# Reading K transposed with odd and even keys alternating, in a grouped-query attention kernel

## The chip, the core and the metric

The kernel runs on one core of one Trainium2 chip. The metric is the device time of one execution in microseconds. A core has five engines that run their own instruction streams and meet at semaphores: TensorE (PE in the profile, with PEld for its weight loads), VectorE (DVE), ScalarE (ACT), GpSimd (POOL) and SyncE (SP), which here issues every DMA. Matmuls write PSUM; the other engines read it and work in SBUF, both 128 partitions wide.

## What is computed

```python
B, Hq, Hkv, Sq, Sk, D = 16, 32, 8, 16, 2048, 128     # q, k, v in bfloat16

def reference(q, k, v):
    rep = Hq // Hkv                                    # 4 query heads share one K/V head
    k = jnp.repeat(k, rep, axis=1)
    v = jnp.repeat(v, rep, axis=1)
    scores = jnp.einsum("bhqd,bhkd->bhqk", q, k) * D ** -0.5
    p = jax.nn.softmax(scores, axis=-1)
    return jnp.einsum("bhqk,bhkd->bhqd", p, v)
```

Four query heads of 16 queries meet the same K and V, so each of the 128 K/V heads has 64 query rows against 2048 keys. K and V are 67 MB each and are read once.

## The kernel before

**Tiling.** Two K/V heads make a pair; there are 64 pairs (NP), and every step handles one pair with 128 query rows, 64 of each head. A chunk is eight pairs (1024 query rows), and Q is loaded and transposed by chunks.

**K.** `load_k` brings a pair's K to `Kn` as one 1 MB transfer; six buffers. A partition holds 32 neighbouring keys of one head with their 128 values, so partitions 0 to 63 are one head and 64 to 127 the other. VectorE (L294) transposes `Kn` in blocks of 32x32 four-byte words, each of which is two neighbouring bf16 values, into `KT`, in two instructions a pair. `KT` then has, for each 32 partitions (half a head), the 32 word positions of a block down the partitions and the keys along the free side. Counted in words the free side is (t b e a x): eight blocks t, two halves b of the head dimension, e for the even or odd key, and 64 positions (a x). Each word holds the two bf16 values of the contraction, and TensorE takes one of them at a time, so it reads with a step of two elements (4 bytes). Two buffers of `KT`.

**Scores.** For a pair, TensorE does 32 matmuls (L250). Four row groups r of 32 rows work at the same time, each for half a head; four accumulation steps `acc` cover the two halves b and the two values in a word; u picks four of the eight blocks t. Each matmul moves 512 columns of `KT` past 64 columns of weights from `QT` and writes 64 partitions of a PSUM bank. `S_ps` has 2048 f32 columns (four banks), in one buffer.

**Negate, minimum, exp.** VectorE (L310) reads `S_ps`, multiplies by minus the softmax scale, takes the row minimum into `nbias` and writes `Sneg` (f32, two buffers), changing the order from half-then-block to block-then-half in runs of 128. ScalarE (L340) computes exp of `Sneg`, with the row sum in `rowsum`, and writes `P` in bf16 (two buffers). `P` is later handled as four-byte words which must hold the even and the odd key side by side; `Sneg` has 64 even keys and then 64 odd ones, so exp reads one of each by turns, 64 words apart, and writes in order.

**Transposes of P, output.** TensorE transposes the words of `P` (L265) in two halves of four blocks to a ring of three PSUM banks `ST_ps`; ScalarE copies each half to `PT` (L350). TensorE multiplies `PT` with V (L281, 32 matmuls), ScalarE divides by the row sum while it copies the result to an output buffer (L360), and SyncE stores it (L199). The reciprocal of the row sum is VectorE's (L301).

**Q.** GpSimd repeats and rearranges a chunk (L163), TensorE transposes it in four parts (L232) in the same PSUM ring, and ScalarE copies each part to `QT` (L330).

**Order.** The order is written out in `pe_prog` and `act_prog`. For pair p, TensorE issues the scores of p+1, the output of p-3, the transposes of p and, for four pairs of each chunk but the last, a part of the next chunk's Q. ScalarE issues exp of p, the scaled copy of p-3, the two copies of P transposed and then the copy of Q. VectorE issues L310 of p, the reciprocal of p-1 and the two K transposes of p+2. The scores of p+1 wait for `sem_max` of p, since `S_ps` has one buffer, and for the K transposes of p+1; L310 waits for the scores; exp of p waits for L310 of p; the transposes of p wait for exp of p. SyncE issues K loads, V loads four pairs later and stores twelve pairs later in one queue. A K load of pair p waits for the transposes of pair p-6, a V load for the output matmuls of pair p-8. The last pair's V comes in two halves.

## Time and profile before

| | |
|---|---|
| time, median of 3 runs | 347.7 us (347.54 to 348.13) |
| profiled execution, its own time | 347.37 us |
| its span, first to last instruction | 345.6 us |
| mean granted clock of TensorE | 0.989 |
| busy: PE / PEld / DVE / ACT / POOL | 278.7 / 193.2 / 295.8 / 280.4 / 30.3 us |
| moved by DMA | 139.11 MB, mean 403 GB/s |
| scores, matmuls of L250 | 2048, 130.2 us |
| exp, L340 | 64, 159.6 us, mean 2494 ns |

The span runs from the first to the last instruction of the profiled execution; its time is a little longer, and the runs without a profile are listed beside it. Busy time is the time in which an engine had an instruction in it. In the page's groups, each row names the source line, engine and operation, output and inputs with their shapes, the count, busy time and the mean duration of one, and, after the second bar, the idle time of the engine just before these instructions and what ended it. Matmuls overlap, so the mean duration of one is longer than the spacing between them. In a timeline, each row gives the start and the length in us of a run of instructions merged into one.

### The profile page before, as it was taken

The page shows a single profiled execution, that of the slowest core. Times are in us where ns is not written, and L with a number is a line of the kernel's source. Part 1 is how long each engine was busy: PE and PEld are TensorE (multiplying, and loading weights), DVE is VectorE, ACT ScalarE, POOL GpSimd, SP SyncE. Part 2 cuts the span into 40 slices and gives each one's busy share as a digit, 9 for nine tenths or more (in the row PEclk, how much of TensorE's full clock was granted, in tenths as well). Part 3 has the DMA queues.
Part 4 walks back from the last instruction along what each step waited for, and adds up shares of the span by engine and source line. Part 5 has one row for each costly group of instructions (what it writes and reads, how often), then busy time and mean ns, then how long its engine had stood idle before and what let it go on. Part 6 is the DMA issues. An engine that isn't in the chain of part 4 may idle for free.

```text
span 345.6 us, 11109 instructions
## 1 busy us (share of the span) xinstructions
PE 278.7 (81%) x4864; PEld 193.2 (56%) x4864; DVE 295.8 (86%) x320; ACT 280.4 (81%) x353; POOL 30.3 (9%) x15
## 2 busy tenths in 40 slices
PE   0667898898999889898869988778877798687785
PEld 0544665665566656666545665456655566454565
DVE  2399989998999989998879989888898898898970
ACT  1458898889988898898866988878987789778776
POOL 4500031000400012000210003000040000000000
PEclk9989999999999999999998999999999999999999
DMA  7999999999999999999999999999999999999983
GB/s 303 423 418 416 407 417 413 412 416 413 413 416 417 416 416 411 418 415 416 414 414 417 415 414 418 412 417 416 414 417 415 414 416 416 414 418 418 408 338 99
DMA packets 37310, 139.11 MB, mean 403 GB/s; under 512 B 11408, under 2 KB 11408, under 8 KB 29072
## 3 DMA queue, kind: packets, MB, share of 16 engines
q1 hardware_dynamic: 37264, 138.42, 98.9%
q8 instruction: 38, 0.62, 0.7%
q14 instruction: 8, 0.07, 0.0%
HBM read 136.31 MB, written 2.10 MB: 401 GB/s over the span
## 4 chain that ended last, share of the span: by engine, by line
DMA 29%; ACT 22%; PE 17%; DVE 14%; issue 14%; SPq 2%; POOL 1%; ACTq 0%
DMA Kn<-in_k_dram 24%; ACT P L340 14%; PE S_ps L250 9%; DVE Sneg L310 8%; DVE KT L294 6%; ACT PT L350 6%; PE ST_ps L265 5%; DMA out_dram<-O 4%; PE O_ps L281 2%; ACT QT L330 2%; SPq L199 2%; DMA Qn<-in_q_dram 1%; POOL Q L163 1%; ACT O L360 1%; PE S_ps L281 0%
## 5 line engine op out<-in xcount | busy, mean ns | idle before, releaser
L294 DVE STREAM_TRANSPOSE KT<-Kn 128x1024 f32<-128x1024 f32 x128 | 151.3, 1221 | 27.6 <-DMA Kn<-in_k_dram 27.5
L340 ACT ACTIVATE P<-Sneg,nbias 128x2048 bf16<-128x2048 f32 x64 | 159.6, 2494 | 12.8 <-DVE Sneg L310 12.4
L250 PE MATMUL S_ps<-KT,QT 32*64 32x512 bf16 x2048 | 130.2, 390 | 36.8 <-DVE Sneg L310 32.5
L310 DVE TENSOR_SCALAR_CACHE_REDUCE Sneg<-S_ps 128x2048 f32<-128x2048 f32 x64 | 144.7, 2262 | 14.0 <-PE S_ps L250 13.7
L250 PEld LDWEIGHTS S_ps<-KT,QT 32*64 32x64 bf16 x2048 | 61.2, 104 | 85.6 <-issue 48.2
L350 ACT ACTIVATE PT<-ST_ps 128x512 f32<-128x512 f32 x128 | 69.6, 595 | 24.2 <-PE ST_ps L265 24.2
L265 PE MATMUL ST_ps<-ident,P 128*128 128x128 f32 x512 | 70.7, 282 | 16.7 <-ACT P L340 16.4
L281 PEld LDWEIGHTS O_ps<-Vb,PT 128*64 128x64 bf16 x1952 | 56.4, 110 | 26.3 <-issue 26.3
L265 PEld LDWEIGHTS ST_ps<-ident,P 128*128 128x128 f32 x512 | 55.5, 142 | 26.4 <-ACT P L340 24.0
L281 PE MATMUL O_ps<-Vb,PT 128*64 128x128 bf16 x1952 | 66.2, 221 | 0.0
L163 POOL COPY Q<-Qn 128x4096 bf16<-128x4096 bf16 x8 | 28.8, 3600 | 228.1 <-DMA Qn<-in_q_dram 157.6
L330 ACT ACTIVATE QT<-ST_ps 128x1024 bf16<-128x1024 bf16 x32 | 32.7, 1032 | 9.0 <-PE ST_ps L232 9.0
L360 ACT ACTIVATE O<-O_ps,rrec 128x128 bf16<-128x128 f32 x61 | 22.5, 370 | 15.0 <-PE O_ps L281 14.8
L232 PE MATMUL ST_ps<-ident,Q 128*128 128x128 bf16 x256 | 20.6, 231 | 10.0 <-POOL Q L163 10.0
L232 PEld LDWEIGHTS ST_ps<-ident,Q 128*128 128x128 bf16 x256 | 18.2, 104 | 10.3 <-issue 9.9
L340 ACT ACTIVATION_READ_ACCUMULATOR P<-Sneg,nbias 128x1 f32 x64 | 13.0, 203 | 0.0
L301 DVE RECIPROCAL rrec<-rowsum 128x1 f32<-128x1 f32 x64 | 10.1, 158 | 2.8 <-ACT P L340 2.8
L310 DVE DVE_READ_ACCUMULATOR Sneg<-S_ps 128x1 f32 x64 | 5.3, 83 | 0.0
L281 PE MATMUL S_ps<-Vb,PT 128*64 128x128 bf16 x96 | 3.1, 220 | 0.7 <-ACT PT L350 0.7
L281 PEld LDWEIGHTS S_ps<-Vb,PT 128*64 128x64 bf16 x96 | 2.8, 110 | 1.0 <-ACT PT L350 1.0
L360 ACT ACTIVATE O<-S_ps,rrec 128x128 bf16<-128x128 f32 x3 | 1.0, 368 | 1.2 <-PE S_ps L281 1.2
L330 ACT ACT_TABLE_LOAD x1 | 1.3, 1283 | 0.7 <-PEq L375 0.7
(7 smaller groups left out, 1.7 us busy)
## 6 DMA issues: line engine op xcount, KB each, us to landing
Kn<-in_k_dram SPq DMA_DIRECT2D x64, 1024.0 KB, 16.5
Vb<-in_v_dram SPq DMA_DIRECT2D x63, 1024.0 KB, 18.1
Qn<-in_q_dram SPq DMA_DIRECT2D x8, 256.0 KB, 16.0
out_dram<-O SPq DMA_DIRECT2D x64, 32.0 KB, 16.0
Vb<-in_v_dram SPq DMA_DIRECT2D x2, 512.0 KB, 12.5
```

Of the source, the lines that this page charges most:

```text
L163: gp.tensor_copy(Q4[:, :, :, :, :].rearrange("p j b r x -> p (j b) r x"), src.unsqueeze(2).to_broadcast([128, 16, 4, 64]),).then_inc(sem_q ...
L232: ins = pe.transpose(dst[:, 128 * j:128 * (j + 1)], src[:, j, b, e, :], ident[:, :])
L250: ins = pe.matmul(S_ps[64 * g:64 * (g + 1), 512 * (2 * h + u):512 * (2 * h + u + 1)], qt[rows, acc, 128 * i + 64 * g:128 * i + 64 * (g + 1 ...
L265: ins = pe.transpose(dst[:, 128 * t:128 * (t + 1)], P[p % 2][:, 128 * x:128 * (x + 1)], ident4[:, :])
L281: ins = pe.matmul(o_ap(p)[64 * g:64 * (g + 1), :], pt[:, j // 2, j % 2, 64 * g:64 * (g + 1)], Vb[p % NV][:, g, j, :], start=(j == 0), stop ...
L294: dve.transpose(KT[p % NKT][:, :].rearrange("p (t b e a x) -> p x e t b a", t=J // 2, b=2, e=2, x=2)[:, x, :, :, :, :], Kn[p % NK][:, :].b ...
L301: dve.reciprocal(rrec[:, p:p + 1], rowsum[:, p:p + 1]).then_inc(sem_rec, 1)
L310: dve.tensor_scalar(Sneg[p % 2][:, :].rearrange("p (t h x) -> p h t x", t=8, h=2), S_ps[:, :].rearrange("p (h t x) -> p h t x", t=8, h=2), ...
L330: act.activation(QT[c % 2][:, i, :].rearrange("p (a j) -> p a j", j=8), stage_ap(u).bitcast(BF16).rearrange("p (j a) -> p a j", j=8), ACT. ...
L340: act.activation(P[p % 2][:, :].bitcast(BF16).rearrange("p (n y e) -> p n y e", n=16, e=2), Sneg[p % 2][:, :].rearrange("p (n e y) -> p n ...
L350: act.activation(PT[p % NPT][:, 4 * h:4 * (h + 1), :].rearrange("p t q -> p (t q)"), stage_ap(u), ACT.Copy,).then_inc(sem_ev, 1)
L360: act.activation(Osb[p % NO][:, :], o_ap(p), ACT.Copy, scale=rrec[:, p:p + 1]).then_inc(sem_nm, 1)
```

## The change

The scores' matmuls read the same 512 columns in another order, and exp's access patterns become plain. `KT` itself, the weights, the PSUM columns written, L310 and all that follows exp stay as they are.

```diff
-                    kt = KT[p % NKT][:, :].bitcast(BF16).rearrange("p (t b y e) -> p b e t y", t=J // 2, b=2, e=2)
+                    kt = KT[p % NKT][:, :].bitcast(BF16).rearrange("p (t b x y e) -> p b e t y x", t=J // 2, b=2, x=2, e=2)
...
-                                    kt[rows, b, e, 4 * u:4 * (u + 1), :],
+                                    kt[rows, b, e, 4 * u:4 * (u + 1), :, :],
...
                     act.activation(
-                        P[p % 2][:, :].bitcast(BF16).rearrange("p (n y e) -> p n y e", n=16, e=2),
-                        Sneg[p % 2][:, :].rearrange("p (n e y) -> p n y e", n=16, e=2), ACT.Exp,
+                        P[p % 2][:, :].bitcast(BF16), Sneg[p % 2][:, :], ACT.Exp,
                         bias=nbias[:, p:p + 1], scale=-1.0, accum_out=rowsum[:, p:p + 1],
                     ).then_inc(sem_exp, 1)
```

In the matmul's pattern, e is now the bf16 value within a word, y one of 64 positions and x the even or odd key. Before, a block's 128 columns were read in memory order, each 4 bytes after the one before. Now x runs fastest: a column of the even half, the column of the odd half at the same position 256 bytes further on, then back to the next of the even half. The scores come to `S_ps`, and through L310 to `Sneg`, with even and odd keys side by side, and exp reads and writes 2048 neighbouring elements.

## The prediction, made before the changed kernel was run

> **What bounds the kernel now.** I read the page's slices and queues first, then the groups of instructions, then the timeline of single pairs. The slices show the engine clock, the DMA share in tenths and the rate; the queue line gives the bytes.

> ```profile
> PEclk9989999999999999999998999999999999999999
> DMA  7999999999999999999999999999999999999983
> GB/s 303 423 418 416 407 417 413 412 416 413 413 416 417 416 416 411 418 415 416 414 414 417 415 414 418 412 417 416 414 417 415 414 416 416 414 418 418 408 338 99
> ...
> q1 hardware_dynamic: 37264, 138.42, 98.9%
> ```

> From the second slice to the thirty-eighth the 16 DMA engines are never under nine tenths and the rate is 407 to 423 GB/s, at most 2% from its middle. The transfers bound the kernel: 139.11 MB over 64 pairs of heads is 2.17 MB a pair, and at 415 GB/s that is 5.2 us a pair. The engines come next, and close behind:

> ```profile
> L294 DVE STREAM_TRANSPOSE KT<-Kn 128x1024 f32<-128x1024 f32 x128 | 151.3, 1221 | 27.6 <-DMA Kn<-in_k_dram 27.5
> L340 ACT ACTIVATE P<-Sneg,nbias 128x2048 bf16<-128x2048 f32 x64 | 159.6, 2494 | 12.8 <-DVE Sneg L310 12.4
> L250 PE MATMUL S_ps<-KT,QT 32*64 32x512 bf16 x2048 | 130.2, 390 | 36.8 <-DVE Sneg L310 32.5
> L310 DVE TENSOR_SCALAR_CACHE_REDUCE Sneg<-S_ps 128x2048 f32<-128x2048 f32 x64 | 144.7, 2262 | 14.0 <-PE S_ps L250 13.7
> ...
> L350 ACT ACTIVATE PT<-ST_ps 128x512 f32<-128x512 f32 x128 | 69.6, 595 | 24.2 <-PE ST_ps L265 24.2
> ...
> L330 ACT ACTIVATE QT<-ST_ps 128x1024 bf16<-128x1024 bf16 x32 | 32.7, 1032 | 9.0 <-PE ST_ps L232 9.0
> L360 ACT ACTIVATE O<-O_ps,rrec 128x128 bf16<-128x128 f32 x61 | 22.5, 370 | 15.0 <-PE O_ps L281 14.8
> ```

> What to see is the waiting columns: the K transposes wait 27.5 us for K loads. Under that lies a loop between two engines. S_ps has one buffer, so the scores of pair p+1 (L250) start only when L310 has read those of pair p, and L310 of p+1 only when they are written:

> ```profile
> 98.67 2.25 DVE L310 TENSOR_SCALAR_CACHE_REDUCE Sneg<-S_ps 128x2048 f32<-128x2048 f32 x1
> ...
> 101.08 2.00 PE L250 MATMUL S_ps<-KT,QT 32*64 32x512 bf16 x32 [0.35 <-DVE Sneg L310]
> 101.30 2.49 ACT L340 ACTIVATE P<-Sneg,nbias 128x2048 bf16<-128x2048 f32 x1
> ...
> 103.20 2.25 DVE L310 TENSOR_SCALAR_CACHE_REDUCE Sneg<-S_ps 128x2048 f32<-128x2048 f32 x1
> ```

> From one L310 to the next is 4.53 us, of which the scores are 2.00. Call this time of a pair's 32 matmuls T. They run four at a time on different row groups, so T is 8 rounds of 250 ns, each moving 512 columns: 0.488 ns a column. One pair in the trace ran with TensorE's clock at half (0.50 in the window from 182 to 184 us) and shows the loop with a longer T:

> ```profile
> 180.82 3.54 PE L250 MATMUL S_ps<-KT,QT 32*64 32x512 bf16 x32 [1.99 <-DVE Sneg L310]
> ...
> 184.41 2.29 DVE L310 TENSOR_SCALAR_CACHE_REDUCE Sneg<-S_ps 128x2048 f32<-128x2048 f32 x1 [0.81 <-PE S_ps L250]
> ...
> 186.86 2.00 PE L250 MATMUL S_ps<-KT,QT 32*64 32x512 bf16 x32 [0.45 <-DVE Sneg L310]
> ```

> L310 began 0.05 us after the scores ended (184.36), and the next scores began 2.50 us after that end. Whatever T is, the loop is T + 2.50.

> **The change, part by part.** No instruction, wait, transfer or buffer is added, removed or moved. Two access patterns change.

> Exp (L340) loses the step in its read. Its price without it comes from ACT's other rows: 512 elements take 595 ns and 1024 take 1032, so 0.854 ns an element and 158 ns fixed; L360's 128 elements with a per-partition operand take 370, 103 more than 158 + 109. So 2048 elements should take 158 + 103 + 1749 = 2010 ns, against 2494: 484 ns saved in each, 31 us of ACT in all. With the step, exp pays (2494 - 261)/2048 = 1.09 ns an element. All but the last exp are hidden behind the transfers; if that cover went, the loop above, without ACT in it, would be next. The last one lies on the path to the end: from it to the end come L360, L350, L281 and the store, so 0.48 us. The halves of the last V were issued at 327.6 and 328.6 us and took 12.4 to 12.6 to land, so by 341.2; its matmuls, now at 341.83, could start 0.48 earlier and would wait for the second half only from their middle. The saving stands.

> TensorE takes that step. Each matmul moved 128 neighbouring columns 4 bytes apart, in four blocks; now each two neighbouring columns lie 256 bytes apart (128 bf16), and the next two start 4 bytes on. Instructions, columns, weight loads and what lands in PSUM are as many as before, in contiguous order as before. No row shows such a read on TensorE: its other moving operands (identity, V) have no hop. I bound T from the rows:
> - Lower end: the hop is free, T = 2.00 (row L250).
> - Exp pays 0.236 ns an element for the very same hops (256 bytes there and back), 28% over its own rate. As a ratio on TensorE: T = 2.56. As an added price: 0.724 ns a column, T = 2.97.
> - As a floor in absolute time, if one hopped element cannot be had from SBUF faster than exp gets it: 1.09 ns a column, 558 ns a round, T = 4.46.
> - Upper end: the K transposes, which write every second word, take 1221/1024 = 1.19 ns a word: T = 4.88. A hop added whole to today's column, 0.488 + 1.09 = 1.58, would make T = 6.47.

> I take 4.46. The row is of the same pattern in the same memory, and TensorE asks for a column every 0.42 to 0.49 ns, over twice as often as exp's 0.854: an engine that already loses 28% at its pace says the memory, not the engine, sets the time of a hopped element.

> [...]

> **The sum.** A pair in which TensorE also transposes a part of Q (28 of 64 lie between two scores) has more to do between the scores:

> ```profile
> 145.88 1.08 PE L281 MATMUL O_ps<-Vb,PT 128*64 128x128 bf16 x32
> ...
> 146.89 1.09 PE L265 MATMUL ST_ps<-ident,P 128*128 128x128 f32 x8
> 147.82 0.61 PE L232 MATMUL ST_ps<-ident,Q 128*128 128x128 bf16 x8
> 148.49 2.00 PE L250 MATMUL S_ps<-KT,QT 32*64 32x512 bf16 x32
> ```

> The scores before these ended at 145.95, so 2.54 us between scores. A longer T hides the K transposes (2.35 us) and all of ACT (2.01 + 0.20 + 0.37 + 1.09 + 1.03 = 4.70 us against a loop of 7), and nothing of it comes out between scores, since exp is then done before L265 needs it. The first scores start at 14.95. After the last scores end, at 334.79, comes L310's part of the loop, 2.50, to 337.29, and then 8.31 us to the end of the span at 345.6, 7.83 with the shorter exp. So

> span = 14.95 + 64 T + 36 x 2.50 + 28 x 2.54 + 7.83 = 183.9 + 64 T,

> where the transfers do not set it. T = 2.00 gives 312, well under the 345.6 of the transfers: a cover of 33 us. Break-even is T = 2.53, or 316 ns a round, 26% more than now. T = 4.46 gives 469.3. The profiled execution took 347.37 for a span of 345.6, so 1.77 lie around it: 471.1 us. The median of the runs, 347.7, is 0.33 above that execution, which changes nothing here. The K loads wait for the transposes of pair p-6 and so slow down with the loop; nothing waits for them any more.

> **Rivals.**
> - *The hop costs TensorE nothing that shows* (T up to 2.53). For it: matmuls already read with a 4-byte step and take only about 17% more than 213 ns a round, half of the 0.42 to 0.43 us at which the half-clock pair's rounds follow one another. Against it: exp's 28%. Then the transfers stay the bound and only the last exp is saved: 347.37 - 0.48 = 346.9, or 347.2 against the median. Under 0.2% (0.7 us, about what a measurement of this kernel can tell from no change), so no change; it is faster if the earlier evictions also let SyncE, which waits 42.7 us for L360 before its stores, smooth the stream by another 0.3 us.
> - *A price that partly hides*: ratio or added price, T = 2.56 to 2.97, 349.5 to 375.8 us. It decides from 316 ns a round on. For it: TensorE may fetch ahead over the two streams, as each still moves by 4 bytes.
> - *A price over exp's*: the fetch of the hop added to the column, T = 6.47, 599.7 us. Against it: nothing on the page pays that much for one element.
> - *It doesn't do what it says*: exp's 2494 ns come from elsewhere, its function or its SBUF read, and stay. With the rest as forecast, 471.6; with a free hop, 347.7.

> **Chances.** Price per column between 0.8 and 1.2 ns, so T from 3.28 to 4.92, 395.6 to 500.5 us: 0.62, and 471 is its likeliest point. Partly hidden, 348 to 395: 0.14. Dearer, over 500: 0.09. Nothing that shows, with exp unchanged or not: 0.15, of which 0.08 within 0.2% and 0.07 faster. So slower 0.85. The range leaves out the case of no price (0.15) and the upper part of the dearer one (0.05): 350 to 520.

> **What would show it.** Right: L250's busy time more than doubles, one matmul means about 560 to 700 ns instead of 390, L310 waits over 100 us for L250, DMA falls to seven tenths in the slices and about 300 GB/s, exp falls to about 2010 ns and K transposes wait no more for loads. The step on TensorE's price is wrong if one pair's scores last well under 4 us or above 5; if they stay at 2.0 to 2.5, the page keeps its nines in the DMA row and the prediction is wrong altogether. The step on exp is wrong if L340 stays above 2300 ns.

## The result, and the profile after

The changed kernel takes 474.49 us (median of 4 runs, 473.64 to 474.84) against 347.73: a ratio of 1.364, 95% interval 1.362 to 1.366. The forecast was 471.1. The profiled execution took 474.26 us with a span of 472.5.

The slices of the page after, TensorE's clock, the DMA share in tenths and the rate:

```profile
PEclk9878998999999999899999999989999999999899
DMA  8999988888888887888988887888888888783200
GB/s 333 419 416 413 413 316 290 330 307 294 329 294 312 323 322 289 306 309 301 312 329 295 311 344 283 292 340 298 290 343 288 289 331 306 284 317 120 69 7 15
```

The transfers no longer bound the kernel. After the first slice they run at the old rate for four, which fits loads that still find free buffers, then at about 310 GB/s, and all but stop some 45 us before the end. The groups of the same page:

```profile
L250 PE MATMUL S_ps<-KT,QT 32*64 32x512 bf16 x2048 | 288.5, 700 | 20.9 <-DVE Sneg L310 16.0
L310 DVE TENSOR_SCALAR_CACHE_REDUCE Sneg<-S_ps 128x2048 f32<-128x2048 f32 x64 | 146.7, 2292 | 160.3 <-PE S_ps L250 160.3
L294 DVE STREAM_TRANSPOSE KT<-Kn 128x1024 f32<-128x1024 f32 x128 | 150.6, 1215 | 6.9 <-DMA Kn<-in_k_dram 6.9
...
L340 ACT ACTIVATE P<-Sneg,nbias 128x2048 bf16<-128x2048 f32 x64 | 128.5, 2007 | 8.4 <-DVE Sneg L310 8.4
```

The waits have changed places: the K transposes wait 6.9 us for loads instead of 27.5, L310 waits 160.3 us for the scores instead of 13.7. Exp is down from 2494 to 2007 ns, and the scores are up from 130.2 to 288.5 us busy. One pair in the timeline of the changed kernel:

```profile
99.42 4.51 PE L250 MATMUL S_ps<-KT,QT 32*64 32x512 bf16 x32
...
99.95 0.14 PEld L250 LDWEIGHTS S_ps<-KT,QT 32*64 32x64 bf16 x4 [0.40 <-issue]
...
100.49 0.14 PEld L250 LDWEIGHTS S_ps<-KT,QT 32*64 32x64 bf16 x4 [0.40 <-issue]
101.03 0.14 PEld L250 LDWEIGHTS S_ps<-KT,QT 32*64 32x64 bf16 x4 [0.40 <-issue]
...
103.85 1.09 PE L281 MATMUL O_ps<-Vb,PT 128*64 128x128 bf16 x32
103.97 2.29 DVE L310 TENSOR_SCALAR_CACHE_REDUCE Sneg<-S_ps 128x2048 f32<-128x2048 f32 x1 [2.36 <-PE S_ps L250]
...
106.42 1.27 PE L250 MATMUL S_ps<-KT,QT 32*64 32x512 bf16 x8
```

The weight loads of a round (four, one for each row group) follow one another by 0.54 us: that is the spacing of the rounds, 1.055 ns for each of 512 columns. Before the change the loads of a pair run on without a gap, so the spacing is taken from the starts of the matmuls. Of one pair's 32 the first starts at 101.1 us and the last at 102.7 (the line gives count, least, median and longest duration in ns, first and last start):

```profile
L250 PE MATMUL S_ps<-KT,QT x32: 380/382/407, 101.1 to 102.7; 32*64 32x512 bf16 x32
```

Seven steps from the first round to the eighth take 1.6 us; by the starts in the trace a step is 227 ns, 0.44 ns a column. (The 250 ns of the prediction are the 2.00 us of a pair divided by eight. A pair's row lasts seven steps and one whole matmul.) From the scores to the next scores is 7.00 us, of which the row of the scores is 4.51; the next matmuls, those of L281, start 0.08 us before it ends. Is this time of the array or of the memory? A stretch of the same run in which the clock was at half answers. The first line is the windows view (window, busy time of each engine, clock, DMA share, GB/s), the others are the timeline there:

```profile
24.00:26.00 2.00, 2.00 (x20) 0.48 (x12) 0.17 (x1) 0.02 (x1) 0.00 (x0) 0.50 0.99 410
```

```profile
24.19 0.16 PEld L250 LDWEIGHTS S_ps<-KT,QT 32*64 32x64 bf16 x4 [0.38 <-issue]
...
24.73 0.16 PEld L250 LDWEIGHTS S_ps<-KT,QT 32*64 32x64 bf16 x4 [0.38 <-issue]
25.27 0.16 PEld L250 LDWEIGHTS S_ps<-KT,QT 32*64 32x64 bf16 x4 [0.38 <-issue]
```

Still 0.54 us. Before the change, half the clock (0.50 between 182 and 184 us) stretched a round from 227 to some 427 ns:

```profile
181.65 0.21 PEld L250 LDWEIGHTS S_ps<-KT,QT 32*64 32x64 bf16 x4 [0.22 <-issue]
182.08 0.21 PEld L250 LDWEIGHTS S_ps<-KT,QT 32*64 32x64 bf16 x4 [0.22 <-issue]
```

The hopped read is not paced by the array's clock. Nor does other traffic move it: in the trace every round but a pair's first, in all 64 pairs, follows the one before by 540 to 542 ns, with transfers at full rate (410 GB/s from 24 to 26 us) and at the end with next to none (7 GB/s in the last slice but one).

### The profile page after: what moved, and what is told of

Its sections match the earlier page's. It is cut to its first block, busy times and chain, and to the rows that moved or that the text cites. A ratio compares the mean times of both kernels' runs of the same rounds, so it can differ in the third digit from the quotient of the medians.

```text
span 472.5 us, 11109 instructions
## 1 busy us (share of the span) xinstructions
PE 438.1 (93%) x4864; PEld 199.1 (42%) x4864; DVE 297.5 (63%) x320; ACT 250.4 (53%) x353; POOL 30.3 (6%) x15
## 2 busy tenths in 40 slices
DMA packets 37310, 139.11 MB, mean 294 GB/s; under 512 B 11408, under 2 KB 11408, under 8 KB 29072
## 3 DMA queue, kind: packets, MB, share of 16 engines
q1 hardware_dynamic: 37264, 138.42, 79.0%
## 4 chain that ended last, share of the span: by engine, by line
PE 82%; issue 13%; ACT 2%; DVE 1%; DMA 1%; POOL 1%; SPq 0%; ACTq 0%
PE S_ps L250 61%; PE O_ps L281 9%; PE ST_ps L265 8%; PE ST_ps L232 3%; DVE Sneg L310 1%; DMA Qn<-in_q_dram 1%; ACT QT L330 1%; POOL Q L163 1%; ACT PT L349 0%; PE S_ps L281 0%; ACT O L359 0%; ACT P L340 0%; SPq L174 0%; ACTq L358 0%
## 5 line engine op out<-in xcount | busy, mean ns | idle before, releaser
L250 PE MATMUL S_ps<-KT,QT 32*64 32x512 bf16 x2048 | 288.5, 700 | 20.9 <-DVE Sneg L310 16.0
L310 DVE TENSOR_SCALAR_CACHE_REDUCE Sneg<-S_ps 128x2048 f32<-128x2048 f32 x64 | 146.7, 2292 | 160.3 <-PE S_ps L250 160.3
L294 DVE STREAM_TRANSPOSE KT<-Kn 128x1024 f32<-128x1024 f32 x128 | 150.6, 1215 | 6.9 <-DMA Kn<-in_k_dram 6.9
L250 PEld LDWEIGHTS S_ps<-KT,QT 32*64 32x64 bf16 x2048 | 64.6, 107 | 186.7 <-issue 185.8
L340 ACT ACTIVATE P<-Sneg,nbias 128x2048 bf16<-128x2048 f32 x64 | 128.5, 2007 | 8.4 <-DVE Sneg L310 8.4
L359 ACT ACTIVATE O<-O_ps,rrec 128x128 bf16<-128x128 f32 x61 | 22.5, 368 | 177.6 <-PE O_ps L281 177.6
L281 PEld LDWEIGHTS O_ps<-Vb,PT 128*64 128x64 bf16 x1952 | 59.4, 114 | 63.6 <-issue 63.6
L265 PE MATMUL ST_ps<-ident,P 128*128 128x128 f32 x512 | 70.5, 281 | 0.0
L281 PE MATMUL O_ps<-Vb,PT 128*64 128x128 bf16 x1952 | 69.5, 227 | 0.0
L265 PEld LDWEIGHTS ST_ps<-ident,P 128*128 128x128 f32 x512 | 55.3, 142 | 9.0 <-issue 3.8
L330 ACT ACTIVATE QT<-ST_ps 128x1024 bf16<-128x1024 bf16 x32 | 32.6, 1030 | 9.1 <-PE ST_ps L232 9.1
L232 PE MATMUL ST_ps<-ident,Q 128*128 128x128 bf16 x256 | 20.3, 228 | 10.1 <-POOL Q L163 10.1
L232 PEld LDWEIGHTS ST_ps<-ident,Q 128*128 128x128 bf16 x256 | 17.9, 103 | 10.3 <-issue 10.0
L340 ACT ACTIVATION_READ_ACCUMULATOR P<-Sneg,nbias 128x1 f32 x64 | 13.1, 205 | 0.0
L310 DVE DVE_READ_ACCUMULATOR Sneg<-S_ps 128x1 f32 x64 | 5.3, 83 | 0.0
L281 PE MATMUL S_ps<-Vb,PT 128*64 128x128 bf16 x96 | 3.0, 220 | 0.7 <-ACT PT L349 0.7
L281 PEld LDWEIGHTS S_ps<-Vb,PT 128*64 128x64 bf16 x96 | 2.8, 110 | 1.0 <-ACT PT L349 1.0
```

Of the source, the lines that this page charges most:

```text
L232: ins = pe.transpose(dst[:, 128 * j:128 * (j + 1)], src[:, j, b, e, :], ident[:, :])
L250: ins = pe.matmul(S_ps[64 * g:64 * (g + 1), 512 * (2 * h + u):512 * (2 * h + u + 1)], qt[rows, acc, 128 * i + 64 * g:128 * i + 64 * (g + 1 ...
L265: ins = pe.transpose(dst[:, 128 * t:128 * (t + 1)], P[p % 2][:, 128 * x:128 * (x + 1)], ident4[:, :])
L281: ins = pe.matmul(o_ap(p)[64 * g:64 * (g + 1), :], pt[:, j // 2, j % 2, 64 * g:64 * (g + 1)], Vb[p % NV][:, g, j, :], start=(j == 0), stop ...
L294: dve.transpose(KT[p % NKT][:, :].rearrange("p (t b e a x) -> p x e t b a", t=J // 2, b=2, e=2, x=2)[:, x, :, :, :, :], Kn[p % NK][:, :].b ...
L310: dve.tensor_scalar(Sneg[p % 2][:, :].rearrange("p (t h x) -> p h t x", t=8, h=2), S_ps[:, :].rearrange("p (h t x) -> p h t x", t=8, h=2), ...
```

## The experiments

**Which half of the change does it?** Exp alone, TensorE as before:

```diff
-                        P[p % 2][:, :].bitcast(BF16).rearrange("p (n y e) -> p n y e", n=16, e=2),
-                        Sneg[p % 2][:, :].rearrange("p (n e y) -> p n y e", n=16, e=2), ACT.Exp,
+                        P[p % 2][:, :].bitcast(BF16), Sneg[p % 2][:, :], ACT.Exp,
```

> The kernel before with exp reading plainly and TensorE reading as before (the keys of a block then stand in another order in P, so the output isn't the reference's). My account: exp falls from 2494 to about 2010 ns, all of it hidden behind the transfers but the last one, so 0.3 to 0.6 us less than before, about 347.2; DMA row still at nine tenths. Rival (exp's time counts in the steady state): 64 times 0.48 is 31 us, so anything under 340.

347.18 us, ratio 0.9978 (0.9968 to 0.9987). Its groups:

```profile
L250 PE MATMUL S_ps<-KT,QT 32*64 32x512 bf16 x2048 | 132.3, 395 | 48.8 <-DVE Sneg L310 42.8
...
L340 ACT ACTIVATE P<-Sneg,nbias 128x2048 bf16<-128x2048 f32 x64 | 128.4, 2007 | 16.5 <-DVE Sneg L310 16.3
```

31 us less work for ScalarE bring 0.2%: ScalarE's work is covered. The 0.63 us between the medians fit the last exp, which I had expected to count, but the two profiled executions do not show it by itself: there the last exp takes 2.00 us in place of 2.46, starts 0.35 us later, and the spans are 345.5 and 345.6 us.

And the other half, the changed kernel with exp's step put back (the same lines the other way round):

> The changed kernel with exp's step put back (keys of P in another order, so the output isn't the reference's). My account: TensorE's read alone makes the loss, and exp, now 2494 ns, is hidden in a loop of 7.0 us but for the last one: 474.5 plus 0.5, so 474.5 to 475.5, scores of a pair still 4.4 to 4.5 us. Rival (the two changes act on each other, ACT and TensorE reading SBUF at once): scores of a pair change by over 0.1 us and the time by over 6 us.

474.13 us, ratio 1.3625 (1.3597 to 1.3652). The scores' busy time is 288.5 us as in the changed kernel, and exp takes 2470 ns. The median lies 0.4 below the lower end expected, well within the spread of the changed kernel's own runs; the loss is TensorE's alone, and the two parts do not act on each other.

**One fetch for all row groups, or one each?** Only row groups 0 and 1 hop:

```diff
-                                    kt[rows, b, e, 4 * u:4 * (u + 1), :, :],
+                                    kt[rows, b, e, 4 * u:4 * (u + 1), :, :] if r < 2 else kp[rows, b, e, 4 * u:4 * (u + 1), :],
```

Here `kp` is the old view of `KT`. Its line moves the later ones down by one, so L250 becomes L251.

> The changed kernel with the alternating read in two of the four row groups only, the other two read as before (half of the keys in another order). If each row group has its own fetch from SBUF at one hopped column in about 1.055 ns, the round still ends with the slow ones: 540 ns a round, scores of a pair about 4.4 us, time about 474. If the four share one fetch, whose time adds up, the round falls to the middle of 250 and 540, 395 ns: scores 3.2 us, about 387 to 395.

```profile
L251 PE MATMUL S_ps<-KT,QT 32*64 32x512 bf16 x2048 | 288.2, 553 | 18.5 <-DVE Sneg L311 13.8
```

```profile
208.01 4.50 PE L251 MATMUL S_ps<-KT,QT 32*64 32x512 bf16 x32 [0.46 <-DVE Sneg L311]
...
212.44 1.08 PE L282 MATMUL O_ps<-Vb,PT 128*64 128x128 bf16 x32
```

In the timeline the scores again take 4.43 us to the next matmuls, as in the changed kernel. The mean of one matmul on the page, 553 ns, is near 545, the middle of 390 and 700, as if one half lasted as before the change and the other as in the changed kernel. The weight loads say the same: they still follow one another by 0.54 us, and the last two rounds of a pair have two each instead of four, so two row groups are done while the other two go on:

```profile
210.71 0.13 PEld L251 LDWEIGHTS S_ps<-KT,QT 32*64 32x64 bf16 x2 [0.41 <-issue]
211.25 0.13 PEld L251 LDWEIGHTS S_ps<-KT,QT 32*64 32x64 bf16 x2 [0.41 <-issue]
```

Each row group pays by itself, at the same time as the others, and those that hop set the end. The one time, 479.19 us, is 4.7 above the changed kernel's median. In its trace six loops from scores to scores take 7.20 to 8.52 us in place of 7.00, 5.5 us in all, against four and 1.8 us in the changed kernel; in them the other TensorE work ran at a lower clock (0.953 over the span against 0.971).

**Moving the interleave to where K is transposed.** If the hop is the price, TensorE must be cured by a `KT` with even and odd keys side by side:

```diff
-KT[p % NKT][:, :].rearrange("p (t b e a x) -> p x e t b a", t=J // 2, b=2, e=2, x=2)[:, x, :, :, :, :],
+KT[p % NKT][:, :].rearrange("p (t b a x e) -> p x e t b a", t=J // 2, b=2, e=2, x=2)[:, x, :, :, :, :],
```

with TensorE as before and exp plain.

> Even and odd keys are put next to each other when the K transposes write KT, so TensorE reads with 4 bytes from column to column and exp reads plainly; the transposes write with 16 bytes between words in place of 8. If the price is of the hop in TensorE's read: scores of a pair back at 2.0 us, exp 2010 ns. Then it hangs on the transposes: at 1221 ns as now, the last exp is saved, about 347.2 us; at 1.3 times (1590 ns) the VectorE work of a pair is 5.3 us against 5.2 of the transfers and it takes 350 to 358; if the hop was not the cause, scores stay above 4 us and it takes over 470.

408.55 us, ratio 1.175 (1.171 to 1.179). Its groups:

```profile
L294 DVE STREAM_TRANSPOSE KT<-Kn 128x1024 f32<-128x1024 f32 x128 | 251.9, 2070 | 5.7 <-DMA Kn<-in_k_dram 5.7
L250 PE MATMUL S_ps<-KT,QT 32*64 32x512 bf16 x2048 | 142.5, 418 | 100.5 <-DVE Sneg L310 85.3
```

A pair's scores take 2.00 us in its timeline:

```profile
200.27 2.00 PE L250 MATMUL S_ps<-KT,QT 32*64 32x512 bf16 x32 [1.54 <-DVE Sneg L310]
```

TensorE is cured. But the transposes, which now write every fourth word instead of every second, went from 1221 to 2070 ns, more than the 1590 I had allowed for, and VectorE, which waits for others only 15.6 of the 406.9 us (7.5 for the scores, 5.7 for K loads, 2.4 for exp), became the bound.

**What is it in the read that costs?** My reason for 1.09 ns was that any hopped element costs so much. Four orders of reading take it apart; each changes the pattern of `kt` in L250 as its expectation describes (the last one also the order of `KT`), and the first three carry a test of exp's read, whose time is hidden in these runs. Each ran once.

> Every second column, then the other 64: 8 bytes from column to column, always upward, no hop back and forth; and exp reads pairs crosswise (0, 2, 1, 3: hops of 8 bytes). Columns in another order, so the output isn't the reference's. Three theories. Lines of 16 bytes, a column in the line just read costing nothing: two columns a line, so 2 x 0.49 = 0.98 against 1.055 ns a line, a round of 250 to 275 ns, scores 2.0 to 2.2 us, about 347 us. Pieces of 8 bytes: each column a new one, 540 ns a round, scores 4.4 us, about 474. Turning back and forth costs, not the distance: round 250, about 347. Exp: by lines of 16 bytes 2010 ns (no new line within four), by 8 bytes or by turning 2490.

> As the one with 8 bytes, with 16 bytes from column to column upward (four passes of 32), and exp's crosswise read with hops of 16 bytes (0, 4, 1, 5 ...). Output not the reference's. Lines of 16 bytes and pieces of 8 bytes both: a new one at each column, 540 ns a round, scores 4.4 us, about 474. Turning back and forth: 250 ns a round, about 347 us. Exp: 2490 ns by all three.

> Two neighbouring columns (8 bytes), then a hop of 1 KB to the next of the four blocks, round the four, then the next two; exp hops by 32 bytes. Output not the reference's. Lines or pieces at 1.055 ns for each one newly read: two columns for each, 0.53 ns a column, 270 ns a round, scores 2.2 us, hidden by the transfers, about 347 us. A fixed price for every hop, 0.57 ns over a column's 0.488: 0.77 ns a column, 395 ns a round, scores 3.2 us, about 390. Turning back after every second column costing as much as after each: 540, 474.

> Columns in the order 0, 2, 1, 3, 4, 6, 5, 7: back and forth by 8 bytes inside 16 bytes (KT is laid out with the halves b outermost for it; the transposes write with the same 8 bytes between words). Output not the reference's. Lines of 16 bytes: no new line until four columns are read, 250 ns a round, scores 2.0 us, about 347 us. Pieces of 8 bytes: each column another piece, 540 ns, 474. Turning back and forth: 540, 474. With the run of 8 bytes upward this tells all three apart.

The orders inside 16 bytes (e8) take 347.63 us, with 347.55 for the kernel before on the same chip, and 2.00 us for a pair's scores in the timeline:

```profile
201.55 2.00 PE L250 MATMUL S_ps<-KT,QT 32*64 32x512 bf16 x32 [0.58 <-DVE Sneg L310]
```

Back and forth by 8 bytes inside 16 costs nothing, and with that neither pieces of 8 bytes nor turning back is the cause. Steps of 16 bytes upward (e6), no turning back in a pass, take 731.57 us, the worst so far:

```profile
201.66 0.13 PEld L250 LDWEIGHTS S_ps<-KT,QT 32*64 32x64 bf16 x4 [0.73 <-issue]
202.56 0.13 PEld L250 LDWEIGHTS S_ps<-KT,QT 32*64 32x64 bf16 x4 [0.77 <-issue]
```

```profile
204.02 0.14 PEld L250 LDWEIGHTS S_ps<-KT,QT 32*64 32x64 bf16 x4 [0.31 <-issue]
204.47 0.14 PEld L250 LDWEIGHTS S_ps<-KT,QT 32*64 32x64 bf16 x4 [0.31 <-issue]
```

```profile
202.01 0.14 PEld L250 LDWEIGHTS S_ps<-KT,QT 32*64 32x64 bf16 x4 [0.30 <-issue]
202.46 0.14 PEld L250 LDWEIGHTS S_ps<-KT,QT 32*64 32x64 bf16 x4 [0.30 <-issue]
```

The first fence is e5's, the second e7's timeline. Over five rounds the spacing is 452 and 444 ns: two columns in 1.77 and 1.73 ns. With lines of 32 bytes e5 would read four columns of a line in a row and e7 still two, and the two would not cost the same. Exp says the same of the line: crosswise by 8 bytes its median is 2004 ns (e5), by 16 bytes 2459 (e6), by 32 bytes 2472 (e7), against 2005 in the changed kernel and 2492 before.

**Why, then, is the change's read cheaper than 1.75 a column?** It visits each line four times, with one other line between. Does a return cost less, and from how far?

> One column from each of four blocks by turns (1 KB apart), then the next column of each: four lines of 16 bytes are visited in turn, each four times in all. Output not the reference's. Single columns from ever new lines took 1.757 ns each (the run with 16 bytes upward), the change's two streams 1.055. If a line read a few columns ago is still at hand, four streams cost as two or a little more: round 540 to 600 ns, 475 to 510 us. If only the one or two lines read last are at hand, every column is a new fetch: round 900 ns, about 730 us.

> Four neighbouring columns (a whole line of 16 bytes), then a hop of 1 KB, round four blocks. Output not the reference's. Price of a new line only: 1.757 ns for four columns is 0.44 ns each, under the 0.488 of today: round 250 ns, scores 2.0 us, about 347 us. A price for the hop itself, on top of the columns: (0.868 - 0.488) x 2 = 0.76 ns for each hop by the run with two columns, 0.19 a column: round 347 ns, scores 2.8 us, about 360.

> Two neighbouring columns from each of two streams by turns (1 KB apart; KT is laid out with the halves b outermost). Output not the reference's. Each line is visited twice. If the second visit needs a fetch again: as the run with two columns and four blocks, 444 ns a round, about 422 us. If the second visit is cheap, as the change's 1.055 ns against 1.757 suggests (a return then costs (4 x 1.055 - 1.757)/3 = 0.82 ns): (1.757 + 2 x 0.42 or so)/4 = 0.65 ns a column, 330 to 350 ns a round, scores 2.65 to 2.8 us, 353 to 364 us.

Each ran once, too. The timelines of e9 (710.57 us) and of e11 (364.73 us):

```profile
206.23 0.13 PEld L250 LDWEIGHTS S_ps<-KT,QT 32*64 32x64 bf16 x4 [0.72 <-issue]
207.10 0.13 PEld L250 LDWEIGHTS S_ps<-KT,QT 32*64 32x64 bf16 x4 [0.74 <-issue]
207.97 0.13 PEld L250 LDWEIGHTS S_ps<-KT,QT 32*64 32x64 bf16 x4 [0.74 <-issue]
```

```profile
206.85 0.14 PEld L250 LDWEIGHTS S_ps<-KT,QT 32*64 32x64 bf16 x4 [0.18 <-issue]
207.17 0.14 PEld L250 LDWEIGHTS S_ps<-KT,QT 32*64 32x64 bf16 x4 [0.19 <-issue]
207.50 0.14 PEld L250 LDWEIGHTS S_ps<-KT,QT 32*64 32x64 bf16 x4 [0.19 <-issue]
207.83 0.14 PEld L250 LDWEIGHTS S_ps<-KT,QT 32*64 32x64 bf16 x4 [0.19 <-issue]
```

With three other lines between, a return costs as much as a new line: 870 ns a round, 1.70 a column. With one between, it is cheap: two streams by pairs take 327 ns a round, 0.639 a column. Put n for a new line, r for a return with one other line between, and nothing for a second column in the same visit. Eight columns of the change are two new lines and six returns, 2n + 6r = 8 x 1.055 = 8.44; eight columns by pairs are 2n + 2r = 5.11. That gives r = 0.83 and n = 1.72 ns, and the second is what four other kernels show directly (1.70, 1.73, 1.76, 1.77). Whole lines with hops of 1 KB (e10) take 347.06 us, against 347.83 for the kernel before (exp reads plainly in e8 to e11), and a pair's scores 2.01 us:

```profile
201.31 2.01 PE L250 MATMUL S_ps<-KT,QT 32*64 32x512 bf16 x32 [0.60 <-DVE Sneg L310]
```

A hop of 1 KB after a whole line costs nothing here. All orders side by side, by the spacing of the rounds:

| columns read, 4 bytes each | kernel | ns a round | ns a column |
|---|---|---|---|
| in order | before | 227 | 0.44 |
| 0, 2, 1, 3 within 16 bytes | e8 | 227 | 0.44 |
| four, then a hop of 1 KB | e10 | 227 | 0.44 |
| two by two from two streams | e11 | 327 | 0.64 |
| two, then a hop, four blocks in turn | e7 | 444 | 0.87 |
| each second | e5 | 452 | 0.88 |
| one by one from two streams | the change | 540 | 1.055 |
| one by one from four streams | e9 | 870 | 1.70 |
| each fourth | e6 | 900 | 1.76 |

The first three rows hold something more. A round in order reads 128 lines, and 227 ns are 1.77 ns a line, the price of a new line once more; half of the 427 ns at half the clock would be only 213. So at full clock even the read in order may wait for its lines rather than for the array. That is an estimate from these numbers; no run separates the two.

**A version that keeps the gain.** Even and odd keys are made neighbours in the transposes, but with the same 8 bytes between written words as before; the two key groups x stay apart until exp, which takes two neighbours from each by turns:

```diff
-kt = KT[p % NKT][:, :].bitcast(BF16).rearrange("p (t b y e) -> p b e t y", t=J // 2, b=2, e=2)
+kt = KT[p % NKT][:, :].bitcast(BF16).rearrange("p (b u y e) -> p b e u y", b=2, u=2, e=2)
...
-kt[rows, b, e, 4 * u:4 * (u + 1), :],
+kt[rows, b, e, u, :],
...
-KT[p % NKT][:, :].rearrange("p (t b e a x) -> p x e t b a", t=J // 2, b=2, e=2, x=2)[:, x, :, :, :, :],
+KT[p % NKT][:, :].rearrange("p (b x t a e) -> p x e t b a", t=J // 2, b=2, e=2, x=2)[:, x, :, :, :, :],
...
-Sneg[p % 2][:, :].rearrange("p (t h x) -> p h t x", t=8, h=2),
-S_ps[:, :].rearrange("p (h t x) -> p h t x", t=8, h=2), -scale, None,
+Sneg[p % 2][:, :].rearrange("p (m h x) -> p h m x", m=16, h=2),
+S_ps[:, :].rearrange("p (h m x) -> p h m x", m=16, h=2), -scale, None,
...
-P[p % 2][:, :].bitcast(BF16).rearrange("p (n y e) -> p n y e", n=16, e=2),
-Sneg[p % 2][:, :].rearrange("p (n e y) -> p n y e", n=16, e=2), ACT.Exp,
+P[p % 2][:, :].bitcast(BF16).rearrange("p (m x e) -> p m x e", x=2, e=2),
+Sneg[p % 2][:, :].rearrange("p (x m e) -> p m x e", x=2, e=2), ACT.Exp,
```

> A version that keeps the gain and avoids the price, with the reference's output: the transposes put the even and the odd key side by side, still with 8 bytes between the words they write, but keep the two key groups x apart, so TensorE reads 512 columns 4 bytes apart in order; exp joins the two groups by reading two neighbours (8 bytes) from each by turns. Scores 2.0 us, transposes 1221 ns as before. [...] The transfers still bound it: like exp reading plainly, 347.1 to 347.4, 0.2% under before; if the transposes or L310 get slower by over a tenth, 350 and more.

347.24 us, ratio 0.9985 (0.9976 to 0.9994):

```profile
L250 PE MATMUL S_ps<-KT,QT 32*64 32x512 bf16 x2048 | 128.4, 386 | 52.0 <-DVE Sneg L310 45.7
...
L340 ACT ACTIVATE P<-Sneg,nbias 128x2048 bf16<-128x2048 f32 x64 | 136.5, 2133 | 16.8 <-DVE Sneg L310 16.6
```

Exp falls to 2133 ns, between the 2494 of before and the 2007 of the plain read, and the scores stay as they were. The time is 0.15% under the kernel before: the interval lies wholly under 1, though the two kernels' single runs overlap (347.18 to 347.77 against 347.33 to 348.54). Exp's 23 us less work in all are covered here as in the run with exp alone.

## Why the prediction was right, point by point

- *What bounds the kernel.* With 31 us taken off ScalarE the time moved by 0.6 us, so ScalarE was not the bound. That the transfers were rests on the DMA row and the rate of the page; no run changed the transfers.
- *Exp without the step.* Forecast 2010 ns from ACT's other rows, measured 2007. Those rows read PSUM and exp reads SBUF; only the result shows that the price carries over.
- *Where the loss sits.* The one-buffer loop between L250 and L310, L310 waiting over 100 us: 160.3. The constant in it, forecast at 2.50 to 2.54 us, came out at 2.49 (103.93 to 106.42).
- *The size of T.* Forecast 4.46 us, measured 4.51, by two errors that nearly cancel. The price of a column was 1.055 ns, not 1.09, and T is not eight rounds: eight of 540 ns are 4.32 us, but a pair's row lasts seven steps of a round and one whole matmul of about 0.70 us. In order, too, eight steps of 227 ns are 1.82 us and the row lasts 2.00. So the read before took 6% over half of the half-clock round, not the 17% that the prediction gives in its first rival.
- *The sum.* The first scores start at 15.03 (forecast 14.95), the last ones at 457.62, and 14.88 us remain (forecast 14.79). The 63 steps between take 7.025 us on average instead of 6.98; that makes 3.0 of the 3.2 us by which the span of 469.3 was short. Of the 0.047 us, about half is in every pair: 7.00 instead of 6.98, a longer T and a smaller constant. The rest comes from four loops at a lower clock, a term I had left out: one, from 70.99 to 78.41, took 7.42 us, its 32 matmuls of L281 1.92 us in place of 1.09, at a clock of 0.53 between 74 and 76 us.
- *The reason for T was only half right.* I took 1.09 ns as what any hopped element costs. There is no such price: a hop inside 16 bytes (e8) and a hop after a whole line (e10) leave a column at 0.44, and a step of 16 bytes with no turning back (e6) costs 1.76. The number held because exp read the same pattern, two lines by turns with four words in each, and for this pattern the two engines come out alike: 1.09 and 1.055 ns. That they do is in part luck. Two by two from two streams cost exp (2133 - 261)/2048 = 0.91 ns an element (e12) and TensorE 0.64 ns a column (e11), so the time of a hopped element is not set by the memory alone, as the prediction had argued. From the same row I would have put the straight step of 16 bytes at 474 us, and it took 731.
- *The rival of a price that partly hides* came near in kind, since part of the price is saved when two streams are read by turns, but not by enough: by the working above a return costs 0.83 ns, nearly twice the 0.44 of a column read in order.
- *DMA at seven tenths* was wrong: the share in the windows of 100 us was 0.84 to 0.86 while the rate, 307 to 309 GB/s, was about as forecast. The share did not fall in step with the rate, and I had divided as if it did. The K transposes still waited 6.9 us for loads, where none had been forecast.

The other orders test the sum with another T. The rows of a pair's scores in e11, e7 and e5, in this order:

```profile
206.53 2.80 PE L250 MATMUL S_ps<-KT,QT 32*64 32x512 bf16 x32
```

```profile
201.14 3.72 PE L250 MATMUL S_ps<-KT,QT 32*64 32x512 bf16 x32
```

```profile
203.13 3.78 PE L250 MATMUL S_ps<-KT,QT 32*64 32x512 bf16 x32
```

183.9 + 64 T + 1.77 gives 364.9, 423.8 and 427.6 us; measured were 364.73, 422.69 and 427.21. For e9 and e6, whose rows last 7.13 and 7.37 us, it gives 642.0 and 657.4, and 710.57 and 731.57 were measured. There the work between the scores of nearly every pair ran at a lower clock (last section), which the sum leaves out.

What stays open is which part of the machine makes a new line cost about twice a return, and what a return costs with two other lines between: three streams were not run. The split into 1.72 and 0.83 ns comes from two equations for two unknowns; only the first value has other runs beside it.

## What to carry to other kernels

Count the lines of 16 bytes that a moving operand touches, in the order in which it touches them, before moving a step from one engine to another: in these runs four bf16 columns at 4 bytes had to come from a line in one visit, or a column took up to four times as long (1.76 ns in place of 0.44), each row group for itself. A step that costs one engine little (exp lost 24%) can cost a faster reader much more (the scores' column went from 0.44 to 1.055 ns), so price it from a row with the very same pattern, and if there is one from the reader itself. And before cheapening an engine, look whether it sets the end: here its 31 us were worth 0.6.

## What the runs showed of the hardware that was not expected

- The transposes on VectorE write every second word at 1.19 ns a word and every fourth at 2.02 (1221 and 2070 ns): the writing side has a price for the step too, between 8 and 16 bytes here. No other step was run.
- In the two runs with the slowest columns TensorE is granted a lower clock, though the profile of e6 has it busy for all of the 300 us from 100 to 400 us: 0.67 over the span with 1.76 ns a column (e6) and 0.70 with 1.70 (e9), against 0.95 to 0.99 in the other runs with a slow read. In each 100 us of e6 from 100 to 400 us the clock was 0.65 to 0.67, and the 32 matmuls of L281 after a pair's scores took 1.92 us in place of 1.09 (the row below). What brings the clock down, no run shows.

```profile
208.07 1.92 PE L281 MATMUL O_ps<-Vb,PT 128*64 128x128 bf16 x32
```
